# Softmax divisors carried by VectorE and DMA in place of GpSimd and TensorE, in a top-k attention and gated-MLP kernel

## The chip, the cores and the metric

The kernel runs on one core of a Trainium2 chip. The metric is the device time of one execution in microseconds (us). The engines are TensorE (PE, with its weight loads shown apart as PEld), VectorE (DVE), ScalarE (ACT), GpSimd (POOL) and SyncE (SP). All engines work through their own instructions in order and wait for one another on semaphores. SP issues nearly every DMA of this kernel, also in order: a DMA that has to wait holds up all that stand behind it on SP.

## The reference

Two blocks in a row, in float32:

```python
# q, k, v: (8 batches, 8 heads, 576 positions, 64)
scores = q @ k.T / 8
kth    = the 32nd largest score of each row
scores = scores where scores >= kth, else -1e9
attn   = exp(scores - max); attn = attn / (attn.sum() + 1e-9)
x      = (attn @ v), as (4608 tokens, 512)
h      = x @ w_in                      # 512 -> 2048
out    = (h * sigmoid(1.702 * h)) @ w_out   # 2048 -> 512
```

What matters here is the division by the sum of a row. The sum belongs to one query of one head, so 128 queries of two heads have 256 divisors.

## The kernel before, in words

**Slots.** Attention is worked off in 144 slots, 18 for each batch. A slot is 128 query rows of two heads (a head pair, `hp`); the last 64 queries of a sequence are put together from two pairs, in two "ends" slots of each batch. Slots 0 to 11 run one by one (`slot`). From slot 12 on, `two_slots(n)` does an iteration for n = 12, 14, 16 and so on, with work of several slots in it. This text calls it iteration n. The order in which every engine gets its work is the order written in these functions; no scheduler changes it.

**One slot's way.** TensorE makes the scores (`scores`, s_ps, L282). ScalarE copies them to SBUF (`copy_scores`, sc, L294). VectorE finds the 32nd largest of each row (`topk_of_pairs`): it takes the greater and the lesser of the two halves of a row (`pair_up`, L323; the lesser on GpSimd, L326 and L327), then lists of eight by MAX8 and MATCH_REPLACE8 (L337, L340), merges two lists of 16 (`merge`, L344), and takes the bound (`cut`, L347). GpSimd makes a second bound (`lows`, L368). ScalarE makes the exponentials and their sums (`exponentials`, L388, L391). ScalarE splits the words of the result into halves (`split`, L462), SP writes them to DRAM (rows, L464) and reads them back transposed (`turn_by_dma`, pt, L470). TensorE multiplies by the values (`values_at`, o, L530), which gives an output with the head dimension along the partitions and the queries along the free axis, not divided yet. ScalarE copies it to SBUF (x, L908) and GpSimd multiplies it by the inverse sums (`x_of`, xT, L544).

**The divisors.** `invert` (called in the middle of VectorE's search for slot n) adds 1e-9 to the sums of slots n-3 and n-2 and takes the reciprocals: 4 numbers on each of 128 partitions, one partition for each query. GpSimd then copies each number 64 times along the free axis (wide, L425), and TensorE transposes the two 128 x 128 blocks into the same PSUM tile as the output (`sum_rows`, o, L519), so that each query's number stands in all 64 rows of its head. Four blocks of 128 columns are so copied to SBUF by the one ScalarE copy L908.

**The MLP.** Four finished x tiles of 128 columns are the input of 128 tokens. `hidden` makes four of the 16 blocks of the hidden layer (ph, L580), ScalarE takes tanh (L597) and a copy (h, L600), GpSimd gates (`gate`, L609, L610), and `project` adds into the output (po, L628). An iteration has two `hidden` and two `project`. The second `hidden` stands right after the values on TensorE and takes the oldest tokens of the list `ready`, to which `finish_x` adds when all four x tiles are there.

**The loads of q and k.** The q and k of a later batch are loaded pair by pair (`load_both`, 6 DMAs into the one buffer qk_l), split into halves by ScalarE (`prepare_by_dma`, halves, L240), written to DRAM by 4 DMAs (qk_rows, L244 to L249), and read back transposed (qk_t, L253). `FETCH` and `READY` say how many slots ahead of a batch this is done; `FETCH_1` and `READY_1` are for batch 1 alone.

**SP's order** in iteration n: loads that are due at slot n; rows of slot n-1; the 4 writes of qk_rows, where there are some; out; pt of slot n-1; qk_t; loads that are due at slot n+1; rows of slot n; pt of slot n. The tile pt has two buffers, so that pt of slot m waits until `values_at` has read that of slot m-2.

Lines as in the profile:

Of the kernel before, what the change touches and what calls it, by code (L numbers as in the profile page):

```python
# [9 lines left out]
ALU = mybir.AluOpType  # L10
ENG = mybir.EngineType
F32 = mybir.dt.float32
# [4 lines left out]
DRAM = bass.MemoryType.DRAM  # L17

P = 128
TOPK = 32  # L20
LOWEST = -3.4028234663852886e38
# [9 lines left out]
def kernel(  # L31
# [27 lines left out]
    nc = tc.nc  # L59

    B, H, S, D = q.shape
# [29 lines left out]
    raws = pool("raws", 8)  # L91
# [10 lines left out]
    thp = pool("thp", 5)  # L102
    apart = pool("apart", 4, space=DRAM)
    apart_qk = pool("apart_qk", 2, space=DRAM)
    ps_s = pool("ps_s", 2, space=PSUM)
    ps_t = pool("ps_t", 2, space=PSUM)
    ps_h = pool("ps_h", 1, space=PSUM)
# [4 lines left out]
    win = const.tile([P, CC, DFF], F32, name="win")  # L112
    wout = const.tile([P, FC, C], F32, name="wout")


    pieces = [(c, g) for g in range(NG) for c in range(CC)] + [(None, f) for f in range(FC)]
    raw = {}
# [210 lines left out]

    def topk_of_pairs(n):

        top = st[n]["top"] = small.tile([P, 2, TOPK + TOPK // 2], F32, name="top2", tag="top")
        cut = st[n]["cut"] = small.tile([P, 2], F32, name="cut")
        first, few = greater.pop(n), lesser.pop(n)
        left = lefts.tile([P, 2, HALF], F32, name="left2", tag="left")

        def largest(src, r, i):
            nc.vector.max(top[:, i, 8 * r : 8 * r + 8], src[:, i, :])  # L337

        def remove(to, src, r, i):
            nc.vector.match_replace(to[:, i, :], top[:, i, 8 * r : 8 * r + 8], src[:, i, :], LOWEST)  # L340

        def merge():
            rest = top[:, :, TOPK // 2 : TOPK]
            nc.vector.tensor_tensor(out=rest, in0=rest, in1=top[:, :, : TOPK - 1 : -1], op=ALU.max)  # L344

        def bound():
            nc.vector.tensor_reduce(  # L347
                out=cut[:], in_=top[:, :, TOPK // 2 - 1 : TOPK], axis=mybir.AxisListType.X, op=ALU.min, negate=True
            )

        ops = []
        for r in range(TOPK // 8):
            ops += [lambda r=r, i=i: largest(left if r else first, r, i) for i in range(2)]
            if r < TOPK // 8 - 1:
                ops += [lambda r=r, i=i: remove(left, left if r else first, r, i) for i in range(2)]
        ops += [lambda: pair_up(n + 1) if n + 1 < N else None]
        for r in range(TOPK // 8, TOPK * 3 // 16):
            ops += [lambda r=r, i=i: largest(few, r, i) for i in range(2)]
            if r == TOPK // 8:
                ops += [lambda r=r, i=i: remove(few, few, r, i) for i in range(2)]  # L360
        return ops + [merge, bound]

    def lows(n):

        top, cut = st[n]["top"], st[n]["cut"]
        low = st[n]["low"] = small.tile([P, 2], F32, name="low")
        for i in range(2):
            nc.gpsimd.tensor_scalar(  # L368
                low[:, i : i + 1], cut[:, i : i + 1], top[:, i, 0:1], -1.0, op0=ALU.add, op1=ALU.mult
            )  # L370

    def bounds(n):
# [23 lines left out]
    def divide(n):  # L396

        some = small.tile([P, 2], F32, name="some", tag="sums")
        nc.vector.tensor_scalar_add(some[:], st[n]["den"], 1e-9)
        rden = small.tile([P, 2], F32, name="rden", tag="inverse")  # L400
        nc.vector.reciprocal(rden[:], some[:])
        by = st[n]["by"] = xtt.tile([P, 2, P], F32, name="by", tag="xT_t")
        for i in range(2):
            nc.gpsimd.tensor_scalar(by[:, i, :], ident[:], rden[:, i : i + 1], None, op0=ALU.mult)

    sums = {}

# [7 lines left out]
    def invert(n):  # L415

        k = (n + 1) // 2
        if k in sums:
            count = 2 if 2 * k < N else 1
            total = sums[k][:, 0:count, :]  # L420
            nc.vector.tensor_scalar_add(total, total, 1e-9)
            inverse = small.tile([P, 2 * count], F32, name="inverse")
            nc.vector.reciprocal(inverse[:], total.rearrange("p s j -> p (s j)"))
            wide = sums[k] = raws.tile([P, 2, 2, D], F32, name="wide", tag="raw")
            nc.gpsimd.tensor_copy(  # L425
                out=wide[:, 0:count, :, :].rearrange("p s j d -> p (s j) d"),
                in_=inverse[:].unsqueeze(2).to_broadcast([P, 2 * count, D]),
            )

    def turn(n, first, blocks):  # L430
        pr = st[n]["pr"]
# [81 lines left out]
        else:  # L513
            put_off.append(bring)


    def sum_rows(m, to):

        nc.tensor.transpose(to, sums[(m + 1) // 2][:, (m + 1) % 2, :, :], ident[:])  # L519

    def values_at(m, o):

        b, t, hps = slots[m]
        pt = st[m]["pt"]
        for p in range(2 if t == NF else 1):
            cols = slice(p * TAIL, (p + 1) * TAIL) if t == NF else slice(0, P)
            main, tail = vv[b, hps[p]]
            for c in range(NF + 1):
                for j in range(2):
                    nc.tensor.matmul(  # L530
                        o[j * D : (j + 1) * D, cols],
                        lhsT=main[:, j, c, :] if c < NF else tail[:, j, :],
                        rhs=pt[:, MAIN[j] + c if c < NF else NF, cols],
                        start=(c == 0),
                        stop=(c == NF),
                    )
        st[m].clear()

    def x_of(m, o, by):

        b, t, hps = slots[m]
        for p in range(2 if t == NF else 1):
            cols = slice(p * TAIL, (p + 1) * TAIL) if t == NF else slice(0, P)
            nc.gpsimd.tensor_tensor(out=x_at(b, t, hps[p]), in0=o[:, cols], in1=by[:, cols], op=ALU.mult)  # L544
        finish_x(m)
# [109 lines left out]


    READY = (-12, -10, -4, -2)
    READY_1 = (-7, -4, -3, -2)
    FETCH = (-16, -11, -8, -3)
    FETCH_1 = (-12, -6, -3, -2)  # L660
    VALUES = (-1, 1, 1, 3)
    by_slot = dict(enumerate([2, 2, 3, 3, 3, 3, 3, 3, 3, 3, 2, 2]))
    for n in by_slot:
# [178 lines left out]
    def two_slots(n):  # L842

        first, second = [later.pop(m, []) for m in (n, n + 1)]
        live = lambda m: 0 <= m < N
        aside = n < N

        def begin(todo):
            for fn, args in todo:
                if fn is not prepare_by_dma:  # L850
                    fn(*args)

        def prepare_some(todo):
            for fn, args in todo:
                if fn is prepare_by_dma:
                    fn(*args)

        def find(m):
            for i, op in enumerate(topk_of_pairs(m) if live(m) else [lambda: None] * 23):
                op()  # L860
                if i == 8 and m % 2 == 0:
                    invert(m - 2)
                if i > 1 and unfinished:
                    finish_one()

        def project_one():
            if may_project(0):
                project(True)

        def measure(m):  # L870
            if live(m):
                bounds(m)
            gate(aside)

        begin(first)
        measure(n - 1)
        if live(n - 1):
            exponentials(n - 1)
            split(n - 1)
        bring_all()  # L880
        find(n)
        hidden()
        project_one()
        tanh(aside)
        prepare_some(first)
        held = [m for m in (n - 3, n - 2) if live(m) and "rows" in st[m]]
        o = ps_t.tile([P, 2, 2, P], F32, name="o", tag="tp") if held else None
        for i, m in enumerate(held):
            sum_rows(m, o[:, i, 0, :])
        if live(n + 2):  # L890
            scores(n + 2)
            copy_scores(n + 2)
        leave_all()
        for i, m in enumerate(held):
            values_at(m, o[:, i, 1, :])
        if live(n - 1):
            turn_by_dma(n - 1)
        while turns:
            turns.pop(0)()
        if live(n + 3):  # L900
            scores(n + 3)
        begin(second)
        measure(n)
        if live(n):
            exponentials(n)
        if held:
            x = raws.tile([P, 2, 2, P], F32, name="x", tag="raw")
            nc.scalar.copy(out=x[:, 0 : len(held)], in_=o[:, 0 : len(held)])  # L908
            for i, m in enumerate(held):
                x_of(m, x[:, i, 1, :], x[:, i, 0, :])  # L910
        if live(n):
            split(n)
            turn_by_dma(n)
        hidden(ps_t)
        if live(n + 3):
            copy_scores(n + 3)
        tanh(aside)
        prepare_some(second)
        project_one()
        leave_all()  # L920
        find(n + 1)
# [40 lines left out]
```

## Time and profile before

| | |
|---|---|
| median of 3 runs | 1514.19 us (1511.37 to 1517.6) |
| the profiled execution | 1512.53 us |
| its span, first to last instruction | 1510.7 us |
| mean granted TensorE clock | 0.983 |
| busy: PE, DVE, ACT, POOL | 96%, 91%, 78%, 59% |
| wide L425 on POOL | x67, mean 856 ns |
| o<-ident,wide L519 on PE | x133, mean 273 ns (pipelined) |
| x L908 on ACT | x67, mean 572 ns |
| merge L344 on DVE | x132, mean 484 ns |
| 16 DMA engines | 62.1% of the span |

The mean of a matmul counts from its start to its end and overlaps with the next one; what a matmul takes of TensorE's time is better read from the distance between starts. "Idle before" in a line of groups is the time that the engine stood still before these instructions, followed by what ended it. A DMA's time from issue to landing is not the time in which SP is held: SP is held while it issues (about 0.6 us for a plain DMA, 2.5 us for a transposing one) and while it waits.

### The profile page before, as it was taken

The page shows a single profiled execution, that of the slowest core. Times are in us where ns is not written, and L with a number is a line of the kernel's source. Part 1 is how long each engine was busy: PE and PEld are TensorE (multiplying, and loading weights), DVE is VectorE, ACT ScalarE, POOL GpSimd, SP SyncE. Part 2 cuts the span into 40 slices and gives each one's busy share as a digit, 9 for nine tenths or more (in the row PEclk, how much of TensorE's full clock was granted, in tenths as well). Part 3 has the DMA queues.
Part 4 walks back from the last instruction along what each step waited for, and adds up shares of the span by engine and source line. Part 5 has one row for each costly group of instructions (what it writes and reads, how often), then busy time and mean ns, then how long its engine had stood idle before and what let it go on. Part 6 is the DMA issues. An engine that isn't in the chain of part 4 may idle for free. (4 is left out here: it accounts for less than half of the span.)

```text
span 1510.7 us, 31439 instructions
## 1 busy us (share of the span) xinstructions
PE 1443.9 (96%) x10729; PEld 1052.8 (70%) x10729; DVE 1378.1 (91%) x4542; ACT 1171.7 (78%) x1846; POOL 891.1 (59%) x1117
## 2 busy tenths in 40 slices
PE   6789878999999999999999999999999999999998
PEld 5667555767777777767777767777777777777775
DVE  7999989999999999999999999999999999999800
ACT  6998878878878787888878787888878888777720
POOL 3788645666666666666666556666666666656500
PEclk7899989999999999999999999999999999999999
DMA  7451876766858587666767667585776767444520
GB/s 226 134 156 43 196 198 184 190 174 171 188 158 211 149 201 194 159 182 157 210 160 182 167 178 191 159 199 150 196 194 155 192 161 207 140 129 134 133 55 14
DMA packets 533777, 248.35 MB, mean 164 GB/s; under 512 B 465136, under 2 KB 507888, under 8 KB 533616
## 3 DMA queue, kind: packets, MB, share of 16 engines
q1 hardware_dynamic: 533184, 246.05, 62.1%
q8 instruction: 84, 1.38, 0.4%
q14 instruction: 77, 0.63, 0.1%
q10 hardware_dynamic: 432, 0.30, 0.1%
HBM read 45.09 MB, written 105.32 MB: 100 GB/s over the span
## 5 line engine op out<-in xcount | busy, mean ns | idle before, releaser
L580 PEld LDWEIGHTS ph<-xT,win 128*128 128x128 f32 x4096 | 474.3, 192 | 69.7 <-issue 53.7
L628 PE MATMUL po<-wout,th 128*128 128x512 f32 x1152 | 518.5, 593 | 1.5 <-POOL wout L147 1.5
L580 PE MATMUL ph<-xT,win 128*128 128x128 f32 x4096 | 489.6, 277 | 12.0 <-POOL xT L544 12.0
L628 PEld LDWEIGHTS po<-wout,th 128*128 128x128 f32 x1152 | 208.1, 191 | 211.1 <-issue 207.9
L337 DVE MAX8 top<-left 128x8 f32<-128x288 f32 x792 | 325.6, 446 | 0.0
L462 ACT COPY sc<-pr 128x2304 uint16<-128x2304 uint16 x133 | 281.5, 2117 | 2.2
L294 ACT ACTIVATE sc<-s_ps 128x576 f32<-128x576 f32 x288 | 172.0, 653 | 128.9 <-PE s_ps L282 126.7
L544 POOL TENSOR_TENSOR xT<-x 128x128 f32<-128x128 f32 x117 | 51.4, 457 | 332.4 <-DVE top L344 161.3
L340 DVE MATCH_REPLACE8 left<-top,left 128x288 f32<-128x288 f32 x528 | 229.7, 443 | 0.0
L391 ACT ACTIVATE pr<-sc,low 128x576 f32<-128x576 f32 x288 | 220.9, 777 | 0.0
L337 DVE MAX8 top<-lesser 128x8 f32<-128x288 f32 x528 | 214.2, 447 | 0.0
L388 ACT ACTIVATE sc<-sc,cut 128x576 f32<-128x576 f32 x288 | 208.7, 783 | 1.6 <-DVE cut L347 1.3
L327 POOL TENSOR_TENSOR lesser<-lesser,greater 128x576 int32<-128x576 int32 x132 | 186.0, 1409 | 22.2 <-DVE greater L323 12.7
L282 PE MATMUL s_ps<-qk_t 64*128 64x288 f32 (+1 forms) x1280 | 186.3, 437 | 9.8 <-ACT sc L294 9.1
L326 POOL TENSOR_TENSOR lesser<-sc 128x576 int32<-128x576 int32 x132 | 187.5, 1421 | 0.0
L610 POOL TENSOR_TENSOR th<-th,h 128x512 f32<-128x512 f32 x127 | 161.7, 1273 | 10.6
L530 PE MATMUL o<-pt,v_l 128*64 128x128 f32 (+1 forms) x2384 | 146.2, 266 | 10.5 <-DMA pt<-rows 10.4
L530 PEld LDWEIGHTS o<-pt,v_l 128*64 128x64 f32 x2384 | 121.1, 138 | 38.6 <-issue 24.9
L597 ACT ACTIVATE th<-ph 128x512 f32<-128x512 f32 x144 | 86.5, 601 | 73.2 <-PE ph L580 73.0
L323 DVE TENSOR_TENSOR greater<-sc 128x576 f32<-128x576 f32 x132 | 104.4, 791 | 36.7 <-ACT sc L294 28.5
L282 PEld LDWEIGHTS s_ps<-qk_t 64*128 64x128 f32 (+1 forms) x1280 | 101.5, 180 | 51.3 <-issue 21.6
L609 POOL TENSOR_SCALAR th<-th 128x512 f32<-128x512 f32 x127 | 78.8, 620 | 66.2 <-ACT th L597 66.0
(86 smaller groups left out, 1648.0 us busy)
## 6 DMA issues: line engine op xcount, KB each, us to landing
rows<-sc SPq DMA_DIRECT2D x133, 576.0 KB, 3.2
qk_rows<-halves SPq DMA_DIRECT2D x56, 256.0 KB, 2.9
qk_l<-in_q_dram SPq DMA_DIRECT2D x64, 128.0 KB, 2.9
raw<-in_moe_w_in_dram SPq DMA_DIRECT2D x16, 512.0 KB, 5.1
v_l<-in_v_dram SPq DMA_DIRECT2D x32, 256.0 KB, 3.0
raw<-in_moe_w_out_dram SPq DMA_DIRECT2D x16, 512.0 KB, 3.7
out_dram<-ob SPq DMA_DIRECT2D x32, 256.0 KB, 2.9
qk_l<-in_k_dram SPq DMA_DIRECT2D x62, 128.0 KB, 2.9
```

Source lines behind the costliest of these rows:

```text
L282: nc.tensor.matmul(ps[i][rows, c, 0:HALF], lhsT=qT[b, hps[p]][on, cols], rhs=kT[b, hps[p]][on, FIRST[i] + c * HALF : FIRST[i] + (c + 1) * ...
L294: nc.scalar.mul(out=to, in_=ps[i][:, :, 0:HALF], mul=SCALE)
L326: nc.gpsimd.tensor_tensor(out=whole, in0=a.bitcast(I32), in1=b.bitcast(I32), op=ALU.add)
L327: nc.gpsimd.tensor_tensor(out=whole, in0=whole, in1=greater[n][:].bitcast(I32), op=ALU.subtract)
L337: nc.vector.max(top[:, i, 8 * r : 8 * r + 8], src[:, i, :])
L340: nc.vector.match_replace(to[:, i, :], top[:, i, 8 * r : 8 * r + 8], src[:, i, :], LOWEST)
L388: nc.scalar.activation(sc[:, i, :], sc[:, i, :], AF.Prelu, bias=cut[:, i : i + 1], alpha=HUGE)
L391: nc.scalar.activation(pr[:, i * S : (i + 1) * S], sc[:, i, :], AF.Exp, bias=low[:, i : i + 1], accum_out=den[:, i : i + 1],)
L462: nc.scalar.copy(out=halves, in_=pr[:].bitcast(U16).rearrange("p (k h) -> p h k", h=2))
L530: nc.tensor.matmul(o[j * D : (j + 1) * D, cols], lhsT=main[:, j, c, :] if c < NF else tail[:, j, :], rhs=pt[:, MAIN[j] + c if c < NF else ...
L580: nc.tensor.matmul(ph[:, i * tiles * P : (i + 1) * tiles * P], lhsT=win[:, c, f * P : (f + 1) * P], rhs=xT[c], start=(c == 0), stop=(c == ...
L628: nc.tensor.matmul(po[:], lhsT=gT[:, i * P : (i + 1) * P], rhs=wout[:, f, :], start=(f == 0), stop=(f == FC - 1))
```

## The change

- `invert`: the reciprocals go into 4 of the 32 columns of a tile (`inverses`, two of them, set to zero at the start), VectorE transposes that tile in blocks of 32 x 32 (turned), and SP writes it to DRAM (lines), where the 128 numbers of each slot and head become one row.
- `spread` is new. It stands where `sum_rows` stood, behind the q/k halves of the iteration: SP reads from `lines` into SBUF (by), each row repeated on 64 partitions by the DMA's own access pattern.
- `sum_rows` and the copy `wide` are gone. The PSUM tile o and its copy x hold two blocks of 128 columns in place of four; `x_of` takes its second operand from by.
- The two lists are put down so that `merge` can be a TENSOR_REDUCE over pairs in place of a TENSOR_TENSOR; one list is written backwards in place of being read backwards.
- The GpSimd product in `divide` (slots 0 to 10) gets a second, idle operation.
- `READY_1` and `FETCH_1` are changed: of batch 1, pair 1 is made ready at slot 12 instead of 14, pair 2 is fetched at slot 13 instead of 15 and made ready at 14 instead of 15, and pair 3 is fetched at slot 15 instead of 16.

```diff
+    apart_by = pool("apart_by", 2, space=DRAM)
+    inverses = [const.tile([P, 32], F32, name=f"inverse{i}") for i in range(2)]
+    for t in inverses:
+        nc.gpsimd.memset(t[:], 0.0)
...
-        top = st[n]["top"] = small.tile([P, 2, TOPK + TOPK // 2], F32, name="top2", tag="top")
+        top = st[n]["top"] = small.tile([P, 2, 2 * TOPK], F32, name="top2", tag="top")
+        def found(r, i, written=False):
+            if r < TOPK // 8:
+                at = (8 * r + TOPK) % (TOPK + TOPK // 2)
+                return top[:, i, at : at + 8]
+            end = 2 * TOPK - 8 * (r - TOPK // 8) - TOPK
+            return top[:, i, end - 1 : end - 9 : -1] if written else top[:, i, end - 8 : end]
...
         def merge():
-            rest = top[:, :, TOPK // 2 : TOPK]
-            nc.vector.tensor_tensor(out=rest, in0=rest, in1=top[:, :, : TOPK - 1 : -1], op=ALU.max)
+            both = top[:, :, 0:TOPK].rearrange("p i (s k) -> p i k s", s=2)
+            nc.vector.tensor_reduce(
+                out=top[:, :, TOPK + TOPK // 2 :], in_=both, axis=mybir.AxisListType.X, op=ALU.max
+            )
...
-            nc.gpsimd.tensor_scalar(by[:, i, :], ident[:], rden[:, i : i + 1], None, op0=ALU.mult)
+            nc.gpsimd.tensor_scalar(by[:, i, :], ident[:], rden[:, i : i + 1], 1.0, op0=ALU.mult, op1=ALU.mult)
...
-            inverse = small.tile([P, 2 * count], F32, name="inverse")
-            nc.vector.reciprocal(inverse[:], total.rearrange("p s j -> p (s j)"))
-            wide = sums[k] = raws.tile([P, 2, 2, D], F32, name="wide", tag="raw")
-            nc.gpsimd.tensor_copy(
-                out=wide[:, 0:count, :, :].rearrange("p s j d -> p (s j) d"),
-                in_=inverse[:].unsqueeze(2).to_broadcast([P, 2 * count, D]),
-            )
+            inverse = inverses[k % 2]
+            nc.vector.reciprocal(inverse[:, 0:4].rearrange("p (j s) -> p s j", j=2)[:, 0:count, :], total)
+            turned = small.tile([P, 32], F32, name="turned")
+            nc.vector.transpose(turned[:], inverse[:])
+            lines = apart_by.tile([16, 2, P], F32, name="lines")
+            nc.sync.dma_start(lines[:].rearrange("j s (g q) -> g (j s) q", q=32), turned[:])
+            sums[k] = lines, count
+
+    def spread(n):
+        lines, count = sums.pop((n + 1) // 2)
+        by = raws.tile([P, 2, P], F32, name="by", tag="raw")
+        row = lines[0:2, 0:count, :].rearrange("j s q -> j (s q)")
+        nc.sync.dma_start(
+            by[:, 0:count, :].rearrange("p s q -> p (s q)"), row.unsqueeze(1).to_broadcast([2, D, count * P])
+        )
+        return by
...
-    READY_1 = (-7, -4, -3, -2)
+    READY_1 = (-7, -6, -4, -2)
-    FETCH_1 = (-12, -6, -3, -2)
+    FETCH_1 = (-12, -6, -5, -3)
...
-        o = ps_t.tile([P, 2, 2, P], F32, name="o", tag="tp") if held else None
-        for i, m in enumerate(held):
-            sum_rows(m, o[:, i, 0, :])
+        by = spread(held[0]) if held else None
+        o = ps_t.tile([P, 2, P], F32, name="o", tag="tp") if held else None
...
-            x = raws.tile([P, 2, 2, P], F32, name="x", tag="raw")
+            x = raws.tile([P, 2, P], F32, name="x", tag="raw")
             nc.scalar.copy(out=x[:, 0 : len(held)], in_=o[:, 0 : len(held)])
             for i, m in enumerate(held):
-                x_of(m, x[:, i, 1, :], x[:, i, 0, :])
+                x_of(m, x[:, i, :], by[:, (m + 1) % 2, :])
```

## The prediction

> **What bounds the kernel now.** I read the page's busy shares, then the chain that ended last, TensorE's waits, and the timeline of SP around a place where TensorE waits.
>
> ```profile
> PE 1443.9 (96%) x10729; PEld 1052.8 (70%) x10729; DVE 1378.1 (91%) x4542; ACT 1171.7 (78%) x1846; POOL 891.1 (59%) x1117
> ```
>
> TensorE is the fullest engine, but VectorE is close. The chain, in order of time, over one iteration (start, us, what):
>
> ```profile
> 1112.70 3.44 PE po L628 x8
> 1116.14 0.22 PE o L519 x2
> 1116.36 1.17 PE s_ps L282 x8
> 1117.53 2.33 PE o L530 x40
> 1119.86 1.17 PE s_ps L282 x8
> 1121.03 3.77 PE ph L580 x32
> 1124.80 3.44 PE po L628 x8
> 1128.24 3.57 PE ph L580 x32
> 1131.81 3.44 PE po L628 x8
> ```
>
> From one po to the same po of the next iteration (1112.70 to 1131.81) are 19.11 us, all on TensorE, piece against piece. The copies x L908 are 19.0 to 19.2 us apart in two thirds of the iterations from 18 to 140, and near 20.1 in most others. The two divisor transposes L519 hold 0.22 us of that. VectorE is busy 48.91 of 50 us in the stretch 1100 to 1150, so 18.68 of 19.10: it has 0.42 to spare. What stops TensorE (who waits for whom, us, times, longest):
>
> ```profile
> PE ph L580 <- POOL xT L544: 12.0, 16, 0.9
> PE o L530 <- DMA pt<-rows: 10.4, 7, 3.6
> PE s_ps L282 <- ACT sc L294: 9.1, 2, 8.4
> ```
>
> The first two matter from iteration 18 on, the last in iteration 16. The first, in the timeline of iteration 64 (start, us, engine line; idle before in brackets):
>
> ```profile
> 663.80 1.26 SPq L184 DMA_DIRECT2D qk_l<-in_q_dram  x2
> 665.11 0.63 SPq L187 DMA_DIRECT2D qk_l<-in_q_dram  x1
> 665.78 1.28 SPq L184 DMA_DIRECT2D qk_l<-in_k_dram  x2
> 667.10 0.63 SPq L187 DMA_DIRECT2D qk_l<-in_k_dram  x1
> 667.78 0.60 SPq L464 DMA_DIRECT2D rows<-sc  x1
> ...
> 671.28 2.48 SPq L470 DMA_TRANSPOSE pt<-rows  x1
> 671.35 0.57 ACT L908 COPY x<-o 128x512 f32<-128x512 f32 x1
> ...
> 672.00 0.87 POOL L544 TENSOR_TENSOR xT<-x 128x128 f32<-128x128 f32 x2 [6.27 <-ACT x L908]
> 672.51 1.16 PE L580 MATMUL ph<-xT,win 128*128 128x128 f32 x8 [0.80 <-POOL xT L544]
> ```
>
> Here `hidden` takes tokens finished 0.05 us earlier. I paired each `hidden` with the x_of that ends its tokens: from iteration 24 on it is this tight in 15 iterations (24, 28, 32, 56, 60, 64, 68, 92, 96, 100, 104, 128, 132, 136, 140); in the others it lies 16 us or more behind.
>
> **What goes from TensorE and ScalarE.** 133 transposes at 0.11 (0.22 a pair in the chain; the 273 ns of one overlap): -14.6 us. No other engine takes the bound: VectorE's 18.68 lose the merge's wait (next part), against a new period of 18.88. The copy x shrinks from 572 to 372 ns (the form 128x256 occurs once, 372): 0.2 at a tight place unless the second operand is last, 10 x 0.2 = -2.0.
>
> **VectorE and GpSimd.** L344 takes 0.19 us in 71 of 132 cases and 0.82 in the other 61, where it runs beside GpSimd's L327. As a reduction it is like L347, 190 ns, which never shows 0.8: 61 x 0.63 = 38 us of VectorE, 0.56 an iteration. The Trainium skill (VectorE: DVE Perf Modes, Rules for kernel authors) speaks against this: it calls `tensor_reduce` the slowest VectorE operation and advises restructuring. By that rule the saving would be nil, and the total below would not move. The 32 x 32 transpose is not in the trace; between L423 (178 ns, four columns) and MAX8 (446 ns, 288 columns), I take 0.2, near the first as it has 32 columns, 67 times. So VectorE lands near 18.3 an iteration, under 18.88: nothing on the path. Were the reduction and the transpose both at their worst (0.82 twice for 0.48 twice, and 0.45), it would be 19.8 and the bound, +0.7 an iteration. Without wide L425, GpSimd has 57 us more to spare; that hides behind 41% idle. The product in `divide`: 22 at 603 ns; TensorE waits 6.3 for it, but VectorE is busy 147.5 of the 150 us up to 200, so 0 to -2; I take 0. The writing backwards, MAX8 with eight results, I put at 0.
>
> **The two new DMAs.** SP's order becomes rows of n-1, lines, qk_rows, by, out, pt of n-1, and so on. Lines never waits for VectorE (L423 stands 5 us or more ahead of rows at the places below). By waits for lines to land, and behind it on SP wait out, pt, qk_t, the loads and the next rows. Issue holds SP 0.6 each. Landing: 16 KB of v_e takes 2.5 (median), 128 KB of qk_l 2.9; a DMA issued right behind rows lands 3.5 after its issue (the eight places, 3.5 to 4.2). For lines I take 3.3, near the last as it stands there, for by 2.9. So by lands 0.6 + 3.3 + 2.9 = 6.8 after rows is issued; bounds 6.0 and 7.1. The skill (DMA: Bandwidth & Descriptors, Anatomy of one DMA) puts a DMA's fixed cost at 2.0 us, taken on GpSimd's queue; twice that would be an estimated 4.6 after rows, and the total some 10 us lower.
>
> *At the tight places.* x_of starts now 0.65 after x begins. Where there are writes of qk_rows or no loads, by has 9.4 us or lands with x: nothing. Five places have loads ahead of rows. The time there, by against x_of's old start, with SP's own delay (0.8 where one iteration before had qk_rows and then SP caught up; 2.8 where SP is full through the batch's end: 0.6 for by behind the first qk_rows, 1.2 for lines and by with the next, 1.0 for waiting on lines in an iteration without):
> 28: 318.7 + 0.8 + 6.8 - 323.5 = 2.8.
> 56: 587.4 + 2.8 + 6.8 - 593.6 = 3.4.
> 64: 667.8 + 0.8 + 6.8 - 672.0 = 3.4.
> 92: 941.9 + 2.8 + 6.8 - 946.1 = 5.4.
> 100: 1018.7 + 0.8 + 6.8 - 1024.5 = 1.8.
> Sum 16.8; less 1.3, by which TensorE itself is later at 56 and 92 (next item): +15.5. With 6.0 and no delay 5.0; with 7.1, 18.
>
> *pt.* In six slots (42, 50, 78, 86, 114, 122) pt lands 0.04 to 0.31 ahead of the values, and SP has been full since qk_rows: lines fits in the wait for halves ahead of it, by does not. 6 x 0.62 = +3.7; bounds 0 (SP catches up) and 8 (the next group, with 1.0 to 2.1, is reached too). Those 11 places don't get the 0.22: +2.4.
>
> *GpSimd's own queue.* While x_of waits for by, the next lesser (L326, L327), low and gate stand behind it. Gate ends 3.4 us ahead of its po, so only lateness over that counts, in some ten places of the same kind: bounds 0 and 9, I take +2 as most lie below 4.
>
> **The loads of batch 1.** Before, ScalarE waits 5.0 for q/k at 203.27, and TensorE stands 8.4. In the changed order pair 1's halves come in iteration 12, where its loads land at 160.7 (last issue 158.0 + 2.6); ScalarE has them done at 162.8, SP their writes at 165.7 and out at 166.1. Then pt of slot 11 (2.6), two qk_t (2.9 + 2.7) and pair 2's loads (4.0): rows of slot 12 at 178.5 instead of 167.64, pt issued 3.1 later and landed 4.7 after that, 186.3 instead of 175.36: a stall of some 11 us in iteration 14. TensorE then has `hidden` and `project` twice (14.2 and the tight xT: to 206), scores and values of slots 13 and 14, whose pt has landed at 206.5 by the same steps, and reaches the second `hidden` of iteration 16 at 210.9 instead of 208.7; there the clock was low before (the stretch 200 to 210: 0.52) and cost 2. From here on 0, with bounds of -6 (ScalarE's waits shrink too) and +6 (the clock falls for longer). Iteration 20: rows at 243.8 + 7.5 (it lands slower there, 4.26) = 251.3 against an x_of needed by 247.4: +4.5, less the wait for pt of 1.47 behind it: +3, bounds 0 and 5.
>
> **Sum.** -14.6 - 2.0 + 15.5 + 3.7 + 2.4 + 2 + 0 + 3 = +10.0 on the profiled execution's 1512.5: 1522.5. The median of the runs is 1.7 above that execution: **1524 us**.
>
> **Rivals.**
> *Faster: both transfers stay hidden.* Lines lands in 2.5, SP catches up, the places above hold. For it: SP waits 279 us for rows and 188 for TensorE from 250 on, idle time that the new issues can use; rows of slots without loads leave 9.4 us. Against: 3.5 to 4.9 are needed where loads stand ahead. -14.6 - 3.0 (all 15 places) = 1494.9, and 1497 as a median.
> *No change.* The terms of waiting come to half: with 5 for the tight places and the rest halved, -16.6 + 5 + 5.6 = -6.0, so 1508; with 12, 1515.
> *Slower by much: SP becomes the bound.* In the batch ends (slots -4 to +2) rows already waits on SP up to 6.7 us. If each such end loses a further 4 us, six of them: +24, 1548. It decides where SP's delay outgrows the 2.5 us of slack of pt in slots 36 and 90.
> *The change misses its aim:* if merge still shows 0.8 beside L327, VectorE has 18.68 + 0.2 = 18.88, all of the new period; with its 0.16 of waiting for sc before L323 the period is 19.04, and 62 x 0.16 = 10 us of the gain are gone: 1534.
>
> **How the numbers follow.** Over 0.5% (7.6 us, about what a measurement of this kernel can tell from no change): the forecast 0.42 and SP as the bound 0.08 give slower, with 0.02 for VectorE: 0.52. No change has 0.26, hidden transfers 0.22. The likeliest case alone holds 1517 to 1533 (tight places from 9, batch 1 up to +6). The range reaches down to 1498, into the hidden case, and up to 1541.
>
> **What would show it.** L519 and L425 gone, the period 18.9 in the regular iterations; TensorE's wait for xT up from 12 to about 25 us, with POOL L544 waiting for the DMA by; pt waits in the six slots longer by 0.6; L344's successor at 0.2 throughout; the 8.4 us stall moved from 198 to about 175. Wrong, if xT's waits stay near 12: then by is on time and the kernel is faster; wrong the other way, if VectorE or SP shows no idle.

## The result: 10% slower, and the profile after

The changed kernel takes 1671.89 us (median of 4 runs, 1666.27 to 1677.64) where the kernel before took 1515.44 in the same runs (4 runs): a ratio of 1.104, 95% interval 1.099 to 1.108. The profiled execution has a span of 1669.7 us and a mean granted TensorE clock of 0.950 (before: 1510.7 and 0.983). "Slower" was right; +157 us in place of +10 was not.

The busy shares of the changed kernel:

```profile
PE 1478.9 (89%) x10596; PEld 1067.1 (64%) x10596; DVE 1382.3 (83%) x4609; ACT 1161.8 (70%) x1846; POOL 847.3 (51%) x1052
```

Every share has fallen: no engine became the bound. TensorE has 133 instructions fewer and is yet busy 35 us longer, at a lower granted clock. From the chain that ended last (start, us, what; pieces between are left out where dots stand), where before it was TensorE piece against piece:

```profile
1399.32 3.70 PE po L648 x8
...
1406.73 3.82 DMA lines<-turned
1410.64 5.69 DMA by<-lines
...
1417.06 0.41 POOL xT L564
1417.48 1.36 POOL lesser L331
1418.92 1.41 POOL lesser L332
1420.33 0.26 POOL low L382
...
1421.64 3.10 DMA rows<-sc
1424.76 4.50 DMA pt<-rows
...
1431.79 3.78 PE ph L600 x32
```

The two new transfers stand in it, and behind them x_of, the next slot's `lesser` and `low` on GpSimd, and then rows and pt. TensorE's waits (us, times, longest), and three groups of instructions (mean ns of one behind the comma; then the idle time ahead of them and what ended it). L600 is now `hidden`, L648 `project`, L550 `values_at`, L564 `x_of`, L630 the gate, L449 the issue of `by`, L441 that of `lines`:

```profile
PE ph L600 <- POOL xT L564: 66.9, 17, 8.9
PE po L648 <- POOL th L630: 52.0, 27, 5.7
PE o L550 <- DMA pt<-rows: 31.6, 13, 9.7
```

```profile
L564 POOL TENSOR_TENSOR xT<-x,by 128x128 f32<-128x128 f32 x117 | 52.6, 468 | 515.7 <-DMA by<-lines 371.7 <-DVE top L349 45.8 <-ACT h L620 25.6
L356 DVE TENSOR_REDUCE top<-top 128x32 f32<-128x64 f32 x132 | 29.2, 221 | 4.5
L439 DVE STREAM_TRANSPOSE turned<-inverse 128x32 f32<-128x32 f32 x67 | 14.2, 211 | 2.3
```

These three waits of TensorE are 150 us; before they were 12.0 for xT and 10.4 for pt, and there was none for the gate. VectorE's two new instructions cost what was foreseen; GpSimd waits 371.7 us for `by`. Iteration 64, to set beside the timeline of before:

```profile
738.76 0.59 SPq L488 DMA_DIRECT2D rows<-sc  x1
739.45 0.61 SPq L441 DMA_DIRECT2D lines<-turned  x1
741.19 0.36 ACT L927 COPY x<-o 128x256 f32<-128x256 f32 x1
742.27 0.55 SPq L449 DMA_DIRECT2D by<-lines  x1
743.19 4.79 SPq L494 DMA_TRANSPOSE pt<-rows  x1
747.95 1.39 POOL L564 TENSOR_TENSOR xT<-x,by 128x128 f32<-128x128 f32 x2 [10.34 <-DMA by<-lines]
748.46 4.64 PE L600 MATMUL ph<-xT,win 128*128 128x128 f32 x26 [6.91 <-POOL xT L564]
```

`by` is issued 3.5 us behind rows, near the predicted 3.9. But x_of starts 5.7 us after that issue, not 2.9; pt, right behind `by`, holds SP for 4.79 us where it took 2.48; and after its wait TensorE needs 4.64 us for 26 matmuls that took 3.17 before (the whole of a group that the prediction's timeline shows the first 8 of):

```profile
672.51 3.17 PE L580 MATMUL ph<-xT,win 128*128 128x128 f32 x26 [0.80 <-POOL xT L544]
```

Three prices, none of them in the sum. Over the execution: `by` to x_of has a median of 5.68 us; pt right behind `by` takes 4.96 us of SP (64 times), the other 69 take 2.56.

### The profile page after: what moved, and what is told of

Same layout as the page of the kernel before. It is cut to its first block, busy times and chain, and to the rows that moved or that the text cites. A ratio compares the mean times of both kernels' runs of the same rounds, so it can differ in the third digit from the quotient of the medians.

```text
span 1669.7 us, 31465 instructions
## 1 busy us (share of the span) xinstructions
PE 1478.9 (89%) x10596; PEld 1067.1 (64%) x10596; DVE 1382.3 (83%) x4609; ACT 1161.8 (70%) x1846; POOL 847.3 (51%) x1052
## 5 line engine op out<-in xcount | busy, mean ns | idle before, releaser
L648 PE MATMUL po<-wout,th 128*128 128x512 f32 x1152 | 537.3, 611 | 53.8 <-POOL th L630 52.0
L600 PEld LDWEIGHTS ph<-xT,win 128*128 128x128 f32 x4096 | 497.5, 200 | 125.0 <-POOL xT L564 70.3
L600 PE MATMUL ph<-xT,win 128*128 128x128 f32 x4096 | 513.4, 285 | 66.9 <-POOL xT L564 66.9
L648 PEld LDWEIGHTS po<-wout,th 128*128 128x128 f32 x1152 | 214.2, 196 | 279.0 <-issue 217.8
L564 POOL TENSOR_TENSOR xT<-x,by 128x128 f32<-128x128 f32 x117 | 52.6, 468 | 515.7 <-DMA by<-lines 371.7
L328 DVE TENSOR_TENSOR greater<-sc 128x576 f32<-128x576 f32 x132 | 123.8, 938 | 104.9 <-ACT sc L299 96.3
L550 PE MATMUL o<-pt,v_l 128*64 128x128 f32 (+1 forms) x2384 | 148.0, 268 | 31.6 <-DMA pt<-rows 31.6
L630 POOL TENSOR_TENSOR th<-th,h 128x512 f32<-128x512 f32 x127 | 167.9, 1322 | 10.6
L550 PEld LDWEIGHTS o<-pt,v_l 128*64 128x64 f32 x2384 | 122.3, 139 | 61.7 <-DMA pt<-rows 35.2
```

The costliest lines, as they stand in the source:

```text
L550: nc.tensor.matmul(o[j * D : (j + 1) * D, cols], lhsT=main[:, j, c, :] if c < NF else tail[:, j, :], rhs=pt[:, MAIN[j] + c if c < NF else ...
L600: nc.tensor.matmul(ph[:, i * tiles * P : (i + 1) * tiles * P], lhsT=win[:, c, f * P : (f + 1) * P], rhs=xT[c], start=(c == 0), stop=(c == ...
L648: nc.tensor.matmul(po[:], lhsT=gT[:, i * P : (i + 1) * P], rhs=wout[:, f, :], start=(f == 0), stop=(f == FC - 1))
```

## Why: the theory and its rivals

The DMA packets of the trace show how `by` moves: 128 packets of 1 KB start 1.35 us after the issue, and the last ends at 5.23. Their own times add up to 7.35 us in these 3.9 us, so 1.9 are under way at once, each for 57 ns. The source of `by` is `[2, 64 (step 0), 256]`: an outermost dimension of 2. The Trainium skill (DMA: Bandwidth & Descriptors, Rules for kernel authors) has the rule that the prediction overlooked: the access pattern's slowest dimension sets how many DMA engines work, and an outermost dimension under 16, "a leading zero-stride broadcast" for one, confines the whole DMA to at most that many. The 1.9 packets at once agree with it; the experiments with other widths follow below.

- **Theory 1, narrow DMA**: two outer rows make `by` land late and hold what stands behind it.
- **Theory 2, the chain**: two dependent DMAs in SP's order are too long a way at any width.
- Rivals beside the DMAs: the loads of batch 1, and VectorE's edits.

The experiments were made on several chips, whose medians of the kernel before lay between 1508.2 and 1514.8 us. So kernels are compared by their ratio to the kernel before in the same runs; 0.001 is 1.5 us.

## Experiments: what the change costs without its parts

**Merge alone.** The kernel before with the new lists, `merge` as TENSOR_REDUCE and the second operation in `divide`.

> The kernel before with only VectorE's merge as TENSOR_REDUCE, its lists laid out for it, and the second operation in the product of `divide`. All theories of the DMAs: 1500-1516 us, merge at 0.22 us. If the merge or the backward writing costs something that the profile of the changed kernel hides: above 1530.

Measured: 1516.09 us, ratio 1.0004 (0.9991 to 1.0016). VectorE's busy time falls from 1378.1 to 1341.3 us, the merge takes 221 ns, and the time stays: saved time off the path.

**Loads alone.** The kernel before with `READY_1 = (-7, -6, -4, -2)` and `FETCH_1 = (-12, -6, -5, -3)`.

> The kernel before with only READY_1 and FETCH_1 of the change. Predicted: no change, 1508-1521 us, the 8.4 us stall of TensorE moved from 198 to about 175 and some 11 us long.

Measured: 1510.47 us, ratio 1.0011 (0.9998 to 1.0024). The timeline has the new stall:

```profile
185.38 1.12 PE L530 MATMUL o<-pt,v_l 128*64 128x64 f32 x16 [9.02 <-DMA pt<-rows]
```

The stall is in iteration 14, as predicted, and 9.0 us long; from the x of iteration 14 to the next x, 31.0 us have become 21.7. Nothing gained or lost. The merge and the loads are out; the new transpose on VectorE stays in the next kernel.

**Neither DMA.**

```diff
-            nc.sync.dma_start(lines[:]..., turned[:])
...
-        nc.sync.dma_start(by[:, 0:count, :]..., row.unsqueeze(1).to_broadcast([2, D, count * P]))
...
-                x_of(m, x[:, i, :], by[:, (m + 1) % 2, :])
+                x_of(m, x[:, i, :], tenths)
```

> As the kernel with the constant tile of 0.1, and neither `lines` nor `by` is issued (the softmax division is left out from slot 11 on; VectorE still inverts and transposes). All theories of the new DMAs: 1485-1510 us, the gain of the removed transposes alone. If the loads of batch 1 or VectorE's edits are the cause: above 1600.

Measured: 1499.51 us, ratio 0.9891 (0.9870 to 0.9912), which is -16.5 us. So the whole loss is in the two DMAs: 0.1145 of the ratio, 173 us, and VectorE's edits, all still there, are out as a cause. The spans say where it is spent. Both kernels have 10596 matmuls; the changed one has 190.8 us of TensorE idle (span less busy) against 65.3, +125.5, and is busy 1478.9 against 1431.4, +47.5. Together +173.0. The busy shares without the DMAs:

```profile
PE 1431.4 (96%) x10596; PEld 1035.0 (69%) x10596; DVE 1390.8 (93%) x4609; ACT 1160.6 (78%) x1846; POOL 841.4 (56%) x1052
```

## Experiments: the width of `by`

**16 outer rows.** Each reciprocal is written into 8 columns, so that `lines` has 16 filled rows; the DMA then repeats each row 8 times. Place and bytes in SBUF are the same.

```diff
-            nc.vector.reciprocal(inverse[:, 0:4].rearrange("p (j s) -> p s j", j=2)[:, 0:count, :], total)
+            nc.vector.reciprocal(
+                inverse[:, 0:32].rearrange("p (j r s) -> p s j r", j=2, r=8)[:, 0:count, :, :],
+                total.unsqueeze(3).to_broadcast([P, count, 2, 8]),
+            )
...
-        row = lines[0:2, 0:count, :].rearrange("j s q -> j (s q)")
+        row = lines[0:16, 0:count, :].rearrange("j s q -> j (s q)")
...
-            ..., row.unsqueeze(1).to_broadcast([2, D, count * P])
+            ..., row.unsqueeze(1).to_broadcast([16, 8, count * P])
```

> The same numbers, but each of the 4 reciprocals is written into 8 of the 32 columns, so that `lines` has 16 filled rows and the DMA `by` has an outermost dimension of 16 (8 partitions each) in place of 2 (64 partitions each). Theory 1 (narrow DMA: `by` goes through two DMA engines, lands 5.7 us after its issue and holds the transposing DMA behind it): `by` to the start of x_of falls from 5.7 to 3 us, the issue of pt behind `by` from 5.0 to 2.5 us, and the time to 1500-1535 us. Theory 2 (two dependent DMAs in SP's order are too long a way whatever their width): the landing gains at most 1 us and the time stays above 1600.

**4 outer rows**, in the same way (r=2; `[4, 32, count * P]`).

> `by` with an outermost dimension of 4 (each reciprocal in 2 columns, 32 partitions to an outer row) in place of 2 or 16, nothing else changed. If the outermost dimension sets how many DMA engines work: its 128 packets last 2.0 us in place of 3.9 (2 rows) and 0.8 (16 rows), pt's issue behind it falls from 5.0 to about 3, and the time lies between 1544 and 1672, nearer to the first: 1555-1600. If any width under 16 is as bad as 2: 1650 or more.

Measured, with the packets' stretch from the first start to the last end:

| outer rows | packets' stretch | at once | last packet after issue | pt's issue behind `by` | `by` issue to x_of | time | ratio |
|---|---|---|---|---|---|---|---|
| 2 | 3.9 us | 1.9 | 5.23 us | 4.96 us | 5.68 us | 1671.89 | 1.1036 (1.0991 to 1.1081) |
| 4 | 1.7 us | 3.7 | 3.04 us | 2.93 us | 3.74 us | 1557.14 | 1.0317 (1.0295 to 1.0340) |
| 16 | 0.84 us | 8.0 | 2.20 us | 2.73 us | 3.35 us | 1543.85 | 1.0180 (1.0163 to 1.0198) |

Theory 1 holds: the width is worth 0.086, 129 of the 157 us. The time itself came out 9 us above what theory 1 allowed; something is left (below). The 4 rows met their expectation. The number of packets under way follows the outer rows at 2 and 4. The wider kernels also read more different rows of DRAM, each fewer times, but that is not what speeds `by` up: a packet takes 57 ns with 2 rows and still 53 with 16 (0.84 us times 8.0, over 128); more of them run at once.

**`by` that nobody reads**: both DMAs at their places, 2 rows, but x_of multiplies by `tenths`.

> Both new DMAs are issued as before, but x_of multiplies by a constant tile of 0.1 and waits for neither (so the softmax division is left out from slot 11 on). This parts the wait of x_of from SP being held. Theory 1a (GpSimd's in-order queue: x_of waits for `by`, and lesser, low and gate stand behind it): 1500-1545 us, GpSimd's wait for `by` gone, pt behind `by` still 5 us. Theory 1b (SP held by `by`, pt later): at least 1600 us, TensorE's and GpSimd's waits then end with pt.

Measured: 1586.83 us, ratio 1.0473 (1.0446 to 1.0500). Neither theory's number: it lies between, since both costs are large (88 us here, and 85 more where x_of waits as well, 1.1036 against 1.0473). TensorE's longest sum of waits is now pt, and SP shows why:

```profile
PE o L552 <- DMA pt<-rows: 81.4, 34, 11.0
```

```profile
1018.79 0.56 SPq L451 DMA_DIRECT2D by<-lines  x1
1019.45 5.30 SPq L496 DMA_TRANSPOSE pt<-rows  x1
1024.84 0.53 SPq L490 DMA_DIRECT2D rows<-sc  x1
1028.12 2.56 SPq L496 DMA_TRANSPOSE pt<-rows  x1
```

The pt behind `by` takes 5.30 us to issue, the next one 2.56. A transfer whose result nobody waits for costs 0.058 over the kernel without DMAs, 88 us.

**The same with 16 rows.**

> The kernel with `by` on 16 outer rows, but x_of multiplies by a constant tile of 0.1 (so the softmax division is left out from slot 11 on) while both DMAs are issued at their places and SP still waits for `lines`. It parts what is left of the loss (1543.9 against 1499.5) into x_of's wait and SP's delay. By the prediction's own terms (pt +3.7 from SP's 0.6, against 15.5 + 2 for x_of's wait) the price of SP alone is some 4 to 10 us: 1503-1512. If SP's delay is the larger part: above 1520.

Measured: 1503.60 us, ratio 0.9963 (0.9952 to 0.9975). SP's price falls from 88 to 11 us by the ratios (3.8 by the two spans).

**2 rows at another place**: VectorE inverts ahead of its search for slot n, and SP issues `lines` and `by` ahead of rows, so that rows and not pt stands behind `by`. Beside it the same place with 16 rows.

```diff
         measure(n - 1)
+        held = [m for m in (n - 3, n - 2) if live(m) and "rows" in st[m]]
+        invert(n - 2)
+        by = spread(held[0]) if held else None
         if live(n - 1):
             exponentials(n - 1)
             split(n - 1)
...
```

> The early place, but `by` with an outermost dimension of 2 as in the changed kernel. Theory 1 in its weak form (a narrow DMA costs by landing late and by holding the transposing DMA that stands right behind it): here rows stands behind it and SP waits there anyway, so 1500-1525 us. In its strong form (a narrow DMA costs wherever it stands, as it takes two DMA engines for 4 us from the other transfers): above 1550.

> As the kernel with `by` on 16 outer rows, and the inverting moved ahead: VectorE inverts right behind the bound of slot n-1 and ahead of the search for slot n, and SP issues `lines` and then `by` ahead of rows of slot n-1, where SP waits for ScalarE's exponentials. Theory 2 for the rest (what is left of the loss, 1543.9 against 1499.5 without the two DMAs, is the chain of two transfers behind rows): `by` has landed before x begins, GpSimd's wait for it is gone, and the time is 1498-1512 us. If the rest is the DMAs' own traffic and SP's issue time: above 1525.

Measured: 1680.34 us, ratio 1.1127 (1.1094 to 1.1159), with 2 rows, and 1547.13 us, 1.0243 (1.0222 to 1.0264), with 16. The weak form is refuted, the strong one holds. SP's queue with 2 rows, and then with 16:

```profile
1211.78 0.57 SPq L449 DMA_DIRECT2D by<-lines  x1
1212.44 0.42 SPq L488 DMA_DIRECT2D rows<-sc  x1
...
1219.03 2.47 SPq L494 DMA_TRANSPOSE pt<-rows  x1
```

```profile
1214.68 0.57 SPq L452 DMA_DIRECT2D by<-lines  x1
1215.34 0.55 SPq L491 DMA_DIRECT2D rows<-sc  x1
...
1219.33 2.44 SPq L497 DMA_TRANSPOSE pt<-rows  x1
```

Rows itself is issued at once, but what waits for it to land, pt, comes 6.6 us later against 4.0. In the packets, the last of rows' ends 6.08 us after the issue where rows stands behind the 2-row `by` (66 times), and after 2.81 us where it does not. So a narrow DMA delays what stands behind it in the queue, plain or transposing. The packets also show how: of the 128 of rows, 112 end within 2.55 us, as they do elsewhere (2.50), and the last 16, an eighth (in 51 of the 66), start only 4.6 us after the issue, when `by` is nearly through (medians). An eighth is what two of sixteen DMA engines would carry, which is the strong form's reason; the trace does not name a packet's engine. No run issued `by` on another queue, so whether that would help is not shown. The expectation for 16 rows here failed too; that is the next question.

## Experiments: what is left at 16 rows

With 16 rows, 1.0180 against 0.9963 with the same DMAs unread: 33 us for x_of's wait, where the prediction had 15.5 + 2. Compared iteration by iteration (x to x) with the unread kernel, the periods that start at 28, 56, 64, 92 and 100 are 7.0, 5.9, 4.8, 4.5 and 5.5 us longer: 27.7, of 41.4 in these two profiled spans. They are the five places of the prediction. x_of starts there 4.7, 3.5, 3.5, 3.0 and 3.9 us after x has ended, in sum 18.6 (predicted 16.8). So the lateness was right, and its price 1.5 times as high: in these five periods TensorE is idle 18.2 us longer and busy 9.5 us longer. Iteration 28 shows why:

```profile
329.05 0.57 SPq L452 DMA_DIRECT2D by<-lines  x1
331.56 0.86 POOL L567 TENSOR_TENSOR xT<-x,by 128x128 f32<-128x128 f32 x2 [8.66 <-DMA by<-lines]
332.06 5.53 PE L603 MATMUL ph<-xT,win 128*128 128x128 f32 x26 [5.22 <-POOL xT L567]
```

The busy times by stretch (PE, PEld, DVE, ACT, POOL; then the granted clock, the DMA share and GB/s) around it:

```profile
325.00:332.00 7.00, 1.84 (x22) 1.05 (x14) 6.93 (x25) 5.05 (x9) 0.44 (x2) 0.87 0.54 158
332.00:340.00 8.00, 7.93 (x32) 6.52 (x33) 7.76 (x27) 1.07 (x2) 5.77 (x8) 0.68 0.83 205
```

TensorE waits 5.22 us and then works at a granted clock of 0.68: its 26 matmuls take 5.53 us in place of 3.17, another 2.4 us.

**Old loads** with the early place and 16 rows.

> The kernel of the early, 16-row `by`, with READY_1 and FETCH_1 as they were before the change. If the loads of batch 1 cost nothing, as predicted (0, bounds -6 and +6): within 6 us of the other; if the moved loads are part of the loss: at least 6 us faster than it.

Measured: 1546.89 us, ratio 1.0253 (1.0228 to 1.0278), against 1.0243: the loads are not it.

The early place failed, and its trace suggests why: SP now waits for `lines` 67 times (110.6 us in sum) in front of rows, and TensorE waits less for xT (23.3 us against 31.1 with 16 rows at the changed kernel's place) and more for pt (36.5 against 26.8).

**`lines` an iteration earlier**, `by` right behind rows (the diff); and, as a second kernel, `by` ahead of the exponentials and so directly ahead of rows.

```diff
-                if i == 8 and m % 2 == 0:
-                    invert(m - 2)
+                if i == 16 and m % 2 == 1:
+                    invert(m - 1)
...
             split(n - 1)
+        held = [m for m in (n - 3, n - 2) if live(m) and "rows" in st[m]]
+        by = spread(held[0]) if held else None
...
```

> `by` on 16 outer rows; inverting and `lines` moved into the iteration before (behind the 16th step of the search for slot n-1, so that SP issues `lines` behind pt of slot n-2 and ahead of the next iteration's loads), `by` right behind rows of slot n-1. The kernel with the early place put `lines` and its wait between the loads and rows and so only moved the lateness from x_of to rows. If the wait for `lines` in SP's order is what is left of the loss: `by` lands 3.1 us behind the issue of rows where x_of wants it 4.2 behind it, the long periods of 24 to 27 us at iterations 28, 56, 64, 92 and 100 shrink to under 21.5, and the time is 1498-1510 us, faster than both kernels. If the two transfers' issue time (1.2 us an iteration) or their traffic is what is left: 1525 or more.

> As the kernel with `lines` in the iteration before, but `by` directly ahead of rows of slot n-1 in place of behind it. In the former, GpSimd still waited up to 8.2 us for `by`, TensorE up to 2.9 us for xT, and the periods at 28, 56, 64, 92 and 100 were still 1 to 3.9 us longer than without that wait, 9 in sum. Here `by` lands about 1.2 us earlier against rows. If that lateness is what is left: 1500-1507 us, those periods under 20.5, and faster than the kernel before by some 0.4%. If the 0.6 us that rows is later costs as much as is gained: 1510-1516.

Measured: behind rows 1512.08 us (12 runs, 1503.19 to 1515.36), ratio 1.0014 (0.9997 to 1.0031); ahead of rows 1537.10 us, 1.0163 (1.0134 to 1.0191). Both expectations were missed: the first comes level with the kernel before, not ahead of it; the second loses what the first won. TensorE's waits in the first, and then in the second and in the early place:

```profile
PE o L553 <- DMA pt<-rows: 18.5, 10, 8.6
PE ph L603 <- POOL xT L567: 17.1, 16, 2.9
```

```profile
PE o L553 <- DMA pt<-rows: 39.7, 21, 8.9
```

```profile
PE o L553 <- DMA pt<-rows: 36.5, 22, 9.1
```

In the second, SP waits for `lines` 55 times (94.9 us) ahead of rows, in the first 39 times (41.1 us) and behind rows. What SP waits for ahead of rows comes back as a wait for pt. Behind rows, the five places were still 3.9, 1.4, 1.6, 1.4 and 1.0 us longer than in the unread kernel.

**By place**: `lines` as in these two, `by` behind rows as a rule, but between the loads of q and of k where these stand ahead of rows.

```diff
+        by = None
+        for fn, args in first:
+            if fn is load_both and held:
+                load("q", *args)
+                by = by or spread(held[0])
+                load("k", *args)
+            else:
+                begin([(fn, args)])
...
+        if held and by is None:
+            by = spread(held[0])
```

> `by` on 16 outer rows and `lines` in the iteration before; `by` right behind rows, as in the better of the two kernels with that place of `lines`, but in iterations whose loads of q and k stand ahead of rows it is issued between the loads of q and those of k. There the loads hide its landing and rows waits for no `lines`. If what is left at iterations 28, 56, 64, 92 and 100 (3.9, 1.4, 1.6, 1.4 and 1.0 us over the kernel that does not wait for `by`) is its landing behind rows: those periods fall to 19.7-20.0 us, TensorE's wait for xT from 17 to 9 us, and the ratio to before is 0.994-0.998, faster than both kernels. If what is left there is SP's own lateness: no gain over the other, ratio 1.000-1.003.

Measured: 1500.39 us (9 runs, 1497.59 to 1505.35), ratio 0.9946 (0.9928 to 0.9964): faster than both kernels, by 0.5% and 10%. Iteration 28, and the wait for xT in sum:

```profile
317.50 0.59 SPq L444 DMA_DIRECT2D lines<-turned  x1
...
320.19 0.56 SPq L452 DMA_DIRECT2D by<-lines  x1
...
323.99 0.60 SPq L491 DMA_DIRECT2D rows<-sc  x1
...
325.15 0.87 POOL L567 TENSOR_TENSOR xT<-x,by 128x128 f32<-128x128 f32 x2 [4.62 <-ACT x L938]
325.66 3.17 PE L603 MATMUL ph<-xT,win 128*128 128x128 f32 x26 [0.59 <-POOL xT L567]
```

```profile
PE ph L603 <- POOL xT L567: 7.9, 15, 0.6
```

x_of now waits for x, not for `by`; the 26 matmuls take 3.17 us again, and the five periods are 19.68 to 19.69 us, to 0.01 us those of the unread kernel. What was left at these places was `by`'s landing.

## Why the prediction was wrong

In its own order, with the sum of the ratios (times 1512.5 us): -16.5 without the DMAs, +11 for their places on SP at 16 rows, +33 for x_of's wait at 16 rows, +129 for the width: +157.

- **TensorE and the copy x, -14.6 - 2.0**: right in sum, -16.5 measured with every edit but the DMAs; the merge (+0.6) and the loads (+1.7) in it are within the noise. The period in the regular iterations is 18.9 there, as forecast.
- **VectorE**: the prices were right, its load was not. The merge took 221 ns (predicted 190), the transpose 211 (200), and with the merge alone VectorE lost 36.8 us of work (38). But without the DMAs it is busy 1390.8 us, more than before (1378.1): the 1e-9 added ahead of the reciprocals takes 582 ns in place of 209, nearly always beside GpSimd's `lesser`, and `pair_up` 895 in place of 791. So VectorE had 196.7 us of work in 200, some 18.6 of an 18.9 period and not 18.3; it stayed off the path with little room. The Trainium skill's rule against `tensor_reduce` (VectorE: DVE Perf Modes, Rules for kernel authors) did not decide here: the reduction replaced 484 ns on average.
- **Loads of batch 1, 0, and iteration 20, +3**: right, +1.7 (-0.3 to +3.6) by the ratio for the loads; at 16 rows iteration 20 is 2.95 us longer where x_of waits. The foreseen time for pt to land was 186.3; the values it held up began at 185.38.
- **When `by` is issued, 0.6 + 3.3 after rows**: right; `lines` to `by` has a median of 3.06.
- **Landing of `by`, 2.9: the step that failed first.** The term was half of what came. It was taken from the row of qk_l because that also has 128 KB, but the loads of qk_l have 128 outer rows on both sides and `by` reads from 2. x_of starts 5.7 after the issue; with 16 rows, 3.35, and 2.5 at the five tight places.
- **"Issue holds SP 0.6 each", and pt +3.7**: `by` itself did (0.56). What it does to the next transfer on the queue was no term at all: 2.4 us for each of 64 pt, 154 us of SP's time, and 88 us of the kernel's even with nobody reading `by`. The bounds of 0 and 8 came from SP's issue alone. At 16 rows the term is 4 to 11 us, near +3.7, but that is luck: in the six slots named TensorE's waits for pt sum to 6.1 us with the unread DMAs on 16 rows and to 6.8 without DMAs. The two spans differ mainly in iterations 18 to 22 (4.5 us) and 114 (2.4), partly made up elsewhere. Of the 129 us of the width, 77 (88 less 11) come with nobody reading `by`, and 52 with x_of's wait.
- **Tight places, +15.5**: places and lateness right once `by` is wide (18.6 against 16.8), price too low, as a wait was counted at its length. 27.7 were paid, of which 9.5 are TensorE being busy longer, at a granted clock of 0.87 to 0.93 over these periods in place of 1.00.
- **GpSimd's own queue, +2 (0 to 9)**: in the changed kernel TensorE waits 52.0 us for the gate, 27 times, as lesser, low and gate stand behind an x_of that waits up to 16.5 us; at 16 rows it is 4.0 us, 3 times. That the queue carries it is read from the order in the trace, and the chain above has `lesser`, `low` and then the next rows and pt behind a late x_of; no run took x_of out of that queue.
- **The direction** was not luck: at 16 rows, where the five tight places are late as foreseen, the kernel is still 1.8% slower than before. The size was wrong.
- **Range**: its ends were bounds of known terms. A new transfer's shape was an unknown that no end covered; of the rivals, SP as the bound came nearest in kind, but it was put at the batch ends and at 24 us.

## What to carry to other kernels

Before a DMA is costed by its bytes, look at the outermost dimension of both its access patterns: a broadcast from a few rows is a narrow transfer, and repeating the rows in DRAM (here by a wider reciprocal, 352 ns in place of 178, for no extra instruction) widens it. Cost a DMA also by what stands behind it in its queue, and put a dependent pair where other transfers cover its landing but not in front of the transfer on the path. A wait of TensorE of some microseconds can cost more than its length.

## What the runs showed of the hardware

- A transfer of 128 KB from two outer rows, at 1.9 packets at once, delayed the next transfer in its queue even where no data depended on it: the issue of a transposing DMA from 2.56 to 4.96 us, the last packet of a plain 576 KB write from 2.81 to 6.08 us. Of that write's 128 packets 112 were on time.
- TensorE's granted clock can fall after a wait and stay low for the next work: the same 26 matmuls took 3.17 us after waits of 0.59 and 0.80 us, 5.53 after 5.22, 4.64 after 6.91, and 4.79 after 2.85 (iteration 28 with `by` behind rows). The Trainium skill (TensorE: Matmul & The Clock Gate, Part 1: The HAM clock gate) states half the clock after an idle window of about 3.4 us; behind the wait of 5.22 us the granted clock was 0.50 for 4 us and 0.68 over 8 us, which fits, while the wait of 2.85 us was shorter than the window. The length alone does not decide: in the changed kernel two waits of 2.86 us each were followed by 3.17 and by 5.91 us (below), and what decides between them is not shown. Of the 173 us that the DMAs cost, 47.5 are TensorE being busy longer, at a mean granted clock of 0.950 against 0.982.

```profile
701.85 3.17 PE L600 MATMUL ph<-xT,win 128*128 128x128 f32 x26 [2.86 <-POOL xT L564]
```

```profile
1192.77 5.91 PE L600 MATMUL ph<-xT,win 128*128 128x128 f32 x26 [2.86 <-POOL xT L564]
```

- GpSimd's 128 x 128 product by a number per partition took 605 ns with one operation (before) and 372 with a second, idle one (merge alone). The time did not move with it.
